# Which work TensorE takes first, where the float limit runs, and which queue loads q and k

## The chip, the cores and the metric

The kernel runs on one core of a Trainium2 chip. TensorE (PE) multiplies matrices into PSUM. VectorE (DVE), ScalarE (ACT) and GpSimd (POOL) do elementwise work, and SyncE (SP) does nothing here but issue DMAs. Each engine has its own stream of instructions and takes them in the order in which the program lists them; an instruction waits on semaphores until its inputs are there. The metric is the device time in microseconds (us) of one execution; the lower the better.

## The reference, cut to what matters

The input is q, k and v of 8 batches, 8 heads, 576 tokens and 64 dimensions, and four weight matrices in float64.

```python
scores = scale * np.matmul(q, k.transpose(0, 1, 3, 2))
thresh = np.max(scores, axis=-1, keepdims=True) - tau
scores = np.where(scores >= thresh, scores, -1000000000.0)
scores = scores - np.max(scores, axis=-1, keepdims=True)
attn = np.exp(scores)
attn = attn / (np.sum(attn, axis=-1, keepdims=True) + 1e-09)
x = (attn @ v), laid out as (8, 576, 512)

xt = x.transpose(0, 2, 1)
h = np.maximum(xt @ w_tok1, 0.0) @ w_tok2
u = x + h.transpose(0, 2, 1)
h2 = np.maximum(u @ w_ch1, 0.0) @ w_ch2
return u + h2
```

## The kernel before

**Attention.** A batch is called a row, and two heads of it are a pair, so there are 8 rows of 4 pairs, numbered 0 to 31. Pair 6 is the third pair of row 1. A unit is 128 queries with both heads of a pair (18 units a row). For two units at a time PE computes scores (`scores_of_two`, L752) into two large PSUM buffers. DVE takes the maxima (`top`, L765), POOL makes the bias (`shift`, L770), ACT applies threshold and scale (`mask`, L780) and the exponential (`exps`, L790), DVE inverts the sums (`inverse`, L276 and L277), and POOL scales the weights (`scale`, L284). The scaled weights must be transposed. In row 0 PE does that through PSUM banks (`turn`, L299, copied out at L304). From row 1 on DVE transposes blocks of 32 x 32 (`turn_blocks`, L314), and four DMAs a unit move the blocks to their place (`move`, L326). Then PE multiplies with v, three units at a time (`values`, L364 for its first matmuls and L369 for the others), and ACT or DVE copies the result out (L373).

**Loads.** A pair's q and k come in eight DMAs of 72 KB (`load_qk`, L106) into two pairs of buffers, so a load must wait until DVE has transposed the pair two before (`prep`, L269). v comes in one DMA in row 0 (`load_v`, L117) and in four later (L120), and its middle part is split off for `values` (`split_middle`, L340). All these DMAs, the moves, the weight loads (L200), the turns of the output (L847), the stores (L895) and the spills (L482) are issued on SP, one after the other.

**Weights.** float64 becomes float32 during row 0, in 31 pieces. ACT prepares two halves (L215, L217), then comes the float limit, a maximum and a multiplication (`on_vector` part 0, L225), then two bit operations on DVE (L227, L231) and an integer addition on POOL (L239). The raw buffer of a piece is loaded anew only when that addition is done.

**MLP.** When a row's attention is done, PE has its token MLP (L398, L410, L423, with adds on DVE at L434) and one or two groups of its channel MLP (L855, its relu at L860 on ACT or L863 on DVE; L871, copied out at L885 or L891). These small products go through two PSUM banks, and fill PE between the scores and the values of the next row. What is put off is done after the attention by hand-written code with fewer products (L1214).

**The planner.** The order of instructions on each engine is found while the program is built, by a greedy planner (`Scheduler`, L518 on). Each operation has an engine, a planned cost, a rank (a lower one goes first), and the operations that it depends on. `start` gives the earliest time at which an operation could begin by the plan. `pick` (L560) takes, for each engine, the operation that can start first; among those that can start now, the one of the lowest rank:

```python
c = (t, rank, x.index) if t > now + 0.02 else (now, rank, x.index)
```

`transfer` plans DMAs: each takes its issue time on the issuing engine, moves at a planned rate, and lands 1.5 us after. At most eight are in flight. An operation may name a second engine (`other`), and then the engine that could start it earlier gets it. What the planner emits is fixed: on the chip an engine that comes to an instruction whose inputs are late waits there, whatever else could run.

Of the kernel before, what the change touches and what calls it, by code (L numbers as in the profile page):

```python
# [14 lines left out]
ALU = mybir.AluOpType  # L15
# [6 lines left out]
def kernel(  # L22
# [25 lines left out]
    nc = tc.nc  # L48
# [10 lines left out]
    NP = H // 2  # L59
# [156 lines left out]
            else:  # L216
                nc.scalar.activation(out=h2, in_=hi.bitcast(F32), func=AF.Abs)  # L217

    def on_vector(i, part, on=nc.vector):
        if wide(i):  # L220
            dst = pieces[i][0]
            lo, hi, h2 = raws[i]
            bits = dst.bitcast(U32)
            if part == 0:
                on.tensor_scalar(out=h2, in0=h2, scalar1=2.0**-15, scalar2=2.0**16, op0=ALU.max, op1=ALU.mult)  # L225
            elif part == 1:
                nc.vector.tensor_scalar(  # L227
                    out=bits, in0=h2.bitcast(U32), scalar1=3, scalar2=0, op0=ALU.logical_shift_left, op1=ALU.bitwise_or
                )
            else:  # L230
                nc.vector.scalar_tensor_tensor(  # L231
                    out=bits, in0=hi, scalar=0x80000000, in1=bits, op0=ALU.bitwise_and, op1=ALU.bitwise_or
                )
# [262 lines left out]
        nc.vector.tensor_scalar(out=ntau, in0=toff, scalar1=SCALE, scalar2=None, op0=ALU.mult)  # L496

    TOKEN_RANK, TOKEN_AFTER_TOKEN = 1.5, 2.5
    FLIGHT, RATE, LANDING = 8, 214.0, 1.5

    class Op:
# [15 lines left out]
    class Scheduler:  # L517
# [22 lines left out]
        def banked(self, cost, work, on, cost_out, leave, deps=(), rank=5, row=None, rank_out=0, other=None):  # L540
# [3 lines left out]
            y.frees = x  # L544
            return x, y

        def start(self, x, eng):
            t = max([d.landed or d.end + (d.lag if d.eng != eng else 0.0) for d in x.deps] + [0.0])
            if x.dmas and len(self.in_flight) == FLIGHT:
                t = max(t, self.in_flight[0])  # L550
            if x.shared and eng == "dve":
                t = max(t, self.clock["pool"])
            if x.bank:
                frees = [b.free for b in self.banks if b.free is not None]
                if not frees:
                    return None
                t = max(t, min(frees))
            return max(t, self.clock[eng])

        def pick(self, eng):  # L560
            best = None
            now = self.clock[eng]
            held = None
            for x in self.ready[eng]:
                t = self.start(x, eng)
                if t is None:
                    continue
                rank = x.rank
                if rank == TOKEN_RANK and self.last_rank == TOKEN_RANK:
                    rank = TOKEN_AFTER_TOKEN  # L570
                c = (t, rank, x.index) if t > now + 0.02 else (now, rank, x.index)
                if x.rank == 1 and eng == "pe" and self.done < x.plan:
                    held = c, t, x
                    continue
                if best is None or c < best[0]:
                    best = c, t, x
            if held and (best is None or best[0][0] > held[0][0] + 0.3):
                best = held
            return best
# [52 lines left out]
    sched = Scheduler()  # L632
# [3 lines left out]
    def key_op(*key):  # L636
        return keyed.get(key)

    def put(key, x):
        keyed[key] = x  # L640
        return x
# [17 lines left out]
    def put_dv(i, part):  # L659
        before = key_op("pool", 26) if part == 1 and i >= CONV - 2 else None  # L660
        put(
            ("dv", i, part),
            sched.op(
                "dve",
                (0.46, 0.47, 0.62)[part],
                lambda: on_vector(i, part),
                (key_op("ac", i, 1), key_op("dv", i, part - 1), before),
                CR[2],
                other=("pool", 0.64, lambda: on_vector(i, 0, nc.gpsimd)) if part == 0 else None,
                shared=part < 2,  # L670
            ),
        )
# [11 lines left out]

    PREP, LOADS = 0.70, 8

    def rank_of_group(b, p0, g):
        return ((b * NP + p0) // 2) * 3 + g  # L690
# [11 lines left out]
    def make_pair(n):  # L702
        b, p = pairs[n]
        if n:
            ahead = (key_op("prep", n - 2, 0), key_op("prep", n - 2, 1))
            for lo in range(0, LOADS, 2):
                put(
                    ("load", n, lo),
                    sched.op(
                        "sp",  # L710
                        0.9,
                        lambda lo=lo: load_qk(n, (nc.sync,) * 2, range(lo, lo + 2)),
                        ahead,
                        0,
                        after=(key_op("load", n - 1, LOADS - 2),),
                        dmas=(2, 107, 0.45),
                    ),
                )
            slot = last_round(n - 2) if n > 1 else -1
            for which in (1, 0):  # L720
                put(
                    ("prep", n, which),
                    sched.op(
                        "dve",
                        PREP,
                        lambda which=which: prep(n, ((which, 0, S // 32),)),
                        [key_op("load", n, lo) for lo in range(0, LOADS, 2)] + [key_op("S", slot)],
                        3,
                        after=(key_op("prep", n - 1, 0),),
                    ),  # L730
                )
        free = key_op("V", last_values(n - 4)) if n >= VL else None
        if n > 1:
            put(("loadv", n), sched.op("sp", 2.0, lambda: load_v(n), (free,), 0, after=(key_op("loadv", n - 1),), dmas=(4, 70, 0.5) if n >= NP else (1, 280, 0.5)))
        put(("split", n), sched.op("dve" if n >= NP else "pool", 0.25 if n >= NP else 0.5, lambda: split_middle(n), (key_op("loadv", n), free), 2))


# [88 lines left out]
    def make_groups(b, halves):  # L826
        uT = xTs[b]
        reads = []
        for i in range(NOW[b]):
            s = {}  # L830
            n, nt = GR, GR // P
# [67 lines left out]
            if b:  # L899
                turn = sched.op("dve", 1.2, turn_u, have + state["stores"] + state["adds"] + (converted if b == 1 else []), 5)  # L900
                reads.append(turn)
                moved = [sched.op("sp", 1.2, lambda k=k, m=move_u: m(k), (turn,), 1, dmas=(nt, 53, 0.6)) for k in range(4)]
            relus = []
            for j in range(NJ):
                x, y = sched.banked(
# [90 lines left out]
    def make_round(it):  # L996
# [25 lines left out]
        for u in us:  # L1022
            b, p0, t = units[u]
            for h in range(2):
                put(("exp", u, h), sched.op("act", 0.77, lambda u=u, h=h: exps(u, h), (key_op("pre", u, h),), 2, lag=0.3))
            n = sched.op("dve", 0.38, lambda u=u: inverse(u), (key_op("exp", u, 0), key_op("exp", u, 1)), 2)
            s = sched.op("pool", 1.46, lambda u=u: scale(u), (n,), 1)
            deps = [s]
            G = rank_of_group(b, p0, t // GU)
            if not b:  # L1030
                deps += [key_op("V", G - 2) if t % GU == 0 else None, key_op("T", u - 1)]
                for third in range(3):
                    x, y = sched.banked(
                        0.33,
                        lambda bank, u=u, third=third: turn(u, third, bank),
                        "act",
                        0.4,
                        lambda bank, u=u, third=third: turned(u, third, bank, nc.scalar.copy),
                        deps,
                        0,  # L1040
                        other=("dve", 0.5, lambda bank, u=u, third=third: turned(u, third, bank, nc.vector.tensor_copy)),
                    )
                    put(("turned", u, third), y)
                    deps = [x]
                put(("T", u), x)
                if t % GU == GU - 1:
                    make_group(b, p0, t // GU)
                    if t // GU == 2 and p0:
                        rows_due.append(b)
                continue  # L1050
            deps += [key_op("T", u - 1), key_op("M", u - 3)]
            put(("T", u), sched.op("dve", 1.31, lambda u=u: turn_blocks(u), deps, 4))
            put(
                ("M", u),
                sched.op(
                    "sp",
                    2.4,
                    lambda u=u: move(u),
                    (key_op("T", u), key_op("V", G - 2) if t % GU == 0 else None),
                    0,  # L1060
                    after=(key_op("M", u - 1),),
                    dmas=(4, 147, 0.6),
                ),
            )
            if t % GU == GU - 1:
                make_group(b, p0, t // GU)
                if p0 == NP - 2 and t // GU == 2:
                    rows_due.append(b)
# [324 lines left out]
```

## Time and profile before

| | |
|---|---|
| Three runs | 1335.69, 1334.21, 1328.55 us; median 1334.21 us |
| Profiled execution | 1338.39 us; span from the first to the last instruction 1336.6 us |
| Granted TensorE clock, mean | 0.978 of full speed |
| Busy share of the span | PE 94%, DVE 58%, ACT 42%, POOL 30% |
| DMA issues of q and k (L106) on SP | 256 |
| DMA issues of moves (L326) on SP | 504 |
| Float limits (L225) | 26 on POOL, mean 1833 ns; 5 on DVE, mean 923 ns |

The busy shares are means over stages that differ: row 0 with the conversion of the weights until about 190 us, the rows 1 to 7 with MLP work between until about 965 us, and the put-off products until the end. A wait of PE in the profile is the idle time just before an instruction, with what ended it. Where several things were waited for, the profile names the one that came last, and with DMAs that can be a neighbour of the transfer that mattered. PEclk is the granted clock of TensorE as a share of full speed. "SPq" marks instructions of SP's queue, where the duration is that of the issue and not of the transfer.

### The profile page before, as it was taken

To read this page: it belongs to the slowest core of one execution; us is meant where nothing else is said; L and a number is where in the kernel's file an instruction comes from. 1 tells how busy PE (TensorE), PEld (TensorE's weight loads), DVE (VectorE), ACT (ScalarE), POOL (GpSimd) and SP (SyncE) were. 2 spreads that over 40 slices of the span, in tenths; PEclk is the share of its full clock that TensorE was granted. 3 is DMA by queue.
4 is the path that set the end of the run, shared out by engine and by line. 5 is a ranking of instruction groups with operands and counts; after the bars stand their busy time and mean duration, and the time that the engine had idled before them with its cause. 6 is when DMAs were issued, how large, how long until landed. Compare 5 with 4: busy or idle time off the path is not lost.

```text
span 1336.6 us, 21896 instructions
## 1 busy us (share of the span) xinstructions
PE 1255.2 (94%) x7982; PEld 995.2 (74%) x7982; DVE 776.8 (58%) x1418; ACT 567.6 (42%) x1233; POOL 401.7 (30%) x692
## 2 busy tenths in 40 slices
PE   6878979999989999989999999999999999999998
PEld 4555668778657776766776676687988888888887
DVE  5887875374756666774666667664154443444342
ACT  5886654454655465553545446452020211112020
POOL 5987863132332333332332333330000000000100
PEclk7989989999999999998999999999999999999999
DMA  9454775364776676685656576452020201021011
GB/s 169 115 138 106 195 168 138 75 133 119 175 166 127 159 148 141 155 172 116 145 133 141 120 175 148 112 137 83 9 71 17 67 28 32 24 62 26 32 32 32
DMA packets 307195, 145.12 MB, mean 109 GB/s; under 512 B 206672, under 2 KB 299856, under 8 KB 307088
## 3 DMA queue, kind: packets, MB, share of 16 engines
q1 hardware_dynamic: 305216, 143.51, 46.4%
q8 instruction: 63, 1.03, 0.3%
q10 hardware_dynamic: 1872, 0.21, 0.1%
q14 instruction: 44, 0.36, 0.1%
HBM read 47.32 MB, written 13.50 MB: 46 GB/s over the span
## 4 chain that ended last, share of the span: by engine, by line
PE 67%; DVE 9%; SPq 9%; POOL 6%; DMA 5%; issue 2%; ACT 2%; DVEq 0%; ACTq 0%; POOLq 0%
PE bank L871 10%; PE o L1214 10%; PE sc L752 7%; PE bank L855 7%; PE bank L369 6%; PE hx L1214 6%; SPq L326 5%; PE hmm L1214 4%; PE oz L1214 4%; PE hz L1214 4%; PE bank L410 4%; DVE mx L765 3%; PE bank L423 3%; POOL e L284 3%; POOL high L225 2%
## 5 line engine op out<-in xcount | busy, mean ns | idle before, releaser
L284 POOL TENSOR_SCALAR e<-e,rr 128x576 f32<-128x576 f32 x288 | 213.1, 755 | 255.2 <-DVE rr L277 192.0
L780 ACT ACTIVATE e<-sc,bias 128x576 f32<-128x576 f32 x288 | 197.9, 742 | 214.7 <-DVE mx L765 144.6
L765 DVE TENSOR_REDUCE mx<-sc 128x1 f32<-128x576 f32 x288 | 198.0, 746 | 56.5 <-PE sc L752 56.0
L790 ACT ACTIVATE e<-e,ntau 128x576 f32<-128x576 f32 x288 | 220.7, 779 | 0.1
L752 PE MATMUL sc<-kT,qT 64*128 64x192 f32 (+1 forms) x1920 | 174.9, 342 | 18.6 <-ACT e L780 16.8
L314 DVE STREAM_TRANSPOSE T<-e 128x1152 f32<-128x1152 f32 x126 | 171.8, 1369 | 30.9 <-DMA eT<-T 19.9
L871 PEld LDWEIGHTS bank<-wc,g 128*128 128x128 f32 x1536 | 179.0, 193 | 12.6 <-issue 3.9
L855 PE MATMUL bank<-xT,wc 128*128 128x256 f32 x768 | 180.6, 385 | 6.2 <-DVE g L863 5.6
L871 PE MATMUL bank<-wc,g 128*128 128x128 f32 x1536 | 182.2, 276 | 0.8 <-DVE us L885 0.8
L752 PEld LDWEIGHTS sc<-kT,qT 64*128 64x128 f32 (+1 forms) x1920 | 143.9, 181 | 51.1 <-ACT e L780 23.4
L855 PEld LDWEIGHTS bank<-xT,wc 128*128 128x128 f32 x768 | 141.3, 190 | 39.1 <-DVE g L863 9.7
L770 POOL TENSOR_SCALAR bias<-mx,toff 128x1 f32<-128x1 f32 x288 | 78.2, 276 | 242.2 <-DVE mx L765 239.1
L369 PE MATMUL bank<-eT,lv 128*64 128x384 f32 (+1 forms) x1024 | 145.8, 427 | 0.1
L1297 POOL TENSOR_TENSOR us<-us,ut 128x256 f32<-128x256 f32 x27 | 22.4, 844 | 392.9 <-DVE us L1135 392.9
L369 PEld LDWEIGHTS bank<-eT,lv 128*64 128x64 f32 x1024 | 80.6, 143 | 54.9 <-issue 42.3
L423 PE MATMUL bank<-w,a 128*128 128x192 f32 (+1 forms) x256 | 72.7, 418 | 6.8 <-DVE xT L434 5.9
L410 PE MATMUL bank<-x_sb,w 128*128 128x512 f32 (+1 forms) x180 | 74.1, 562 | 0.4 <-ACT eT L304 0.2
L364 PE MATMUL bank<-eT,vl 128*64 128x384 f32 (+1 forms) x256 | 46.1, 438 | 25.2 <-DMA eT<-T 9.1
L1262 ACT ACTIVATE ga<-hmm 128x256 f32<-128x256 f32 x30 | 11.5, 384 | 117.1 <-PE hmm L1214 117.1
L423 PEld LDWEIGHTS bank<-w,a 128*128 128x128 f32 x256 | 42.5, 190 | 23.6 <-DVE xT L434 7.3
L790 ACT ACTIVATION_READ_ACCUMULATOR e<-e,ntau 128x1 f32 x288 | 58.7, 204 | 0.0
L1135 DVE TENSOR_TENSOR temps<-hx,temps 128x256 f32<-128x256 f32 x60 | 25.1, 419 | 56.7 <-PE hx L1214 56.6
(130 smaller groups left out, 1551.7 us busy)
## 6 DMA issues: line engine op xcount, KB each, us to landing
eT<-T SPq DMA_DIRECT2D x504, 144.0 KB, 3.0
lk<-in_k_dram SPq DMA_DIRECT2D x126, 72.0 KB, 3.0
lq<-in_q_dram SPq DMA_DIRECT2D x124, 72.0 KB, 3.1
out_dram<-us SPq DMA_DIRECT2D x32, 256.0 KB, 2.1
ut<-us SPq DMA_DIRECT2D x128, 64.0 KB, 2.1
lv<-in_v_dram SPq DMA_DIRECT2D x112, 72.0 KB, 2.6
spare<-in_moe_w_ch_dram SPq DMA_DIRECT2D x8, 512.0 KB, 3.7
extra<-in_moe_w_ch_dram SPq DMA_DIRECT2D x8, 512.0 KB, 3.8
```

Of the source, the lines that this page charges most:

```text
L284: nc.gpsimd.tensor_scalar(out=eh, in0=eh, scalar1=rr[:, h : h + 1], scalar2=1.0, op0=ALU.mult, op1=ALU.mult)
L314: nc.vector.transpose(out=T.rearrange("p a (c x) -> p c a x", c=NK), in_=e.rearrange("p (c a x) -> p c a x", c=NK, a=4))
L369: nc.tensor.matmul(to[r], lhsT=lv[:, j, :], rhs=e[j], start=False, stop=(c == NI - 1), skip_group_check=True)
L410: nc.tensor.matmul(bank[:, 0 : P * L], lhsT=w1[:, t, P * m : P * m + P], rhs=x_sb[:, t, cols], start=(t == 0), stop=(t == NT - 1))
L423: nc.tensor.matmul(bank[:, n * i : n * i + n], lhsT=hidden[b][:, m, P * c : P * c + P], rhs=w2[:, m, lo : lo + n], start=(m == 0), stop=(m ...
L752: nc.tensor.matmul(sc[h][rows, f, HT * k : HT * k + HT], lhsT=qT[r, cols], rhs=kT[r, HT * f : HT * f + HT], start=True, stop=True, skip_gr ...
L765: nc.vector.tensor_reduce(out=mx[:, h : h + 1], in_=part[h], axis=AX.XY, op=ALU.max)
L780: nc.scalar.activation(out=eh, in_=part[h], func=AF.Prelu, bias=bias[:, h : h + 1], scale=SCALE, alpha=STEEP)
L790: nc.scalar.activation(out=eh, in_=eh, func=AF.Exp, bias=ntau, accum_out=rs[:, h, 0:1])
L855: nc.tensor.matmul(bank[:, 0:n], lhsT=wc1[:, j, c, :], rhs=uT[:, c, GR * i : GR * i + n], start=(c == 0), stop=(c == NCC - 1))
L871: nc.tensor.matmul(to, lhsT=s["g"][:, j, P * t : P * t + P], rhs=wc2[:, j, P * c : P * c + P], start=(j == 0 and b > 0), stop=(j == NJ - 1 ...
L1214: nc.tensor.matmul(ps, lhsT=l, rhs=r, start=start and x == 0, stop=x == len(pairs) - 1, skip_group_check=not start)
```

## The change

1. In `pick`, among the operations that could start now on PE, those that are *sure* go before those that aren't, ahead of the rank. An operation is sure when what it needs lies far enough back in the plan: 1 us (`SLACK`) after the planned end of an operation on another engine, 4 us (`SPARE`) after the planned landing of a DMA, 1 us after the planned release of a PSUM bank.
2. Planned issue times per DMA become longer: 0.58 us for q and k (0.45), 0.67 for v from row 1 on (0.50), 0.645 for moves and for the turns of the output (0.60).
3. The float limit no longer has POOL as its second engine: all 31 are on DVE.
4. From pair 6 on, q and k are loaded by DMAs that ACT issues, two to an operation, at rank 2.5. No ACT operation of the attention has a higher number, so these go last among those that could start now. Earlier pairs stay on SP.

```diff
-    def on_vector(i, part, on=nc.vector):
+    def on_vector(i, part):
...
-                on.tensor_scalar(out=h2, in0=h2, scalar1=2.0**-15, scalar2=2.0**16, op0=ALU.max, op1=ALU.mult)
+                nc.vector.tensor_scalar(out=h2, in0=h2, scalar1=2.0**-15, scalar2=2.0**16, op0=ALU.max, op1=ALU.mult)
...
+    SLACK, SPARE = 1.0, 4.0
...
+        def sure(self, x):
+            t = max([d.landed + SPARE if d.landed else d.end + d.lag + SLACK * (d.eng != x.eng) for d in x.deps] + [0.0])
+            if x.bank:
+                t = max(t, min(b.free for b in self.banks if b.free is not None) + SLACK)
+            return t
...
-                c = (t, rank, x.index) if t > now + 0.02 else (now, rank, x.index)
+                c = t if t > now + 0.02 else now, eng == "pe" and self.sure(x) > now + 0.02, rank, x.index
...
-                other=("pool", 0.64, lambda: on_vector(i, 0, nc.gpsimd)) if part == 0 else None,
...
-    PREP, LOADS = 0.70, 8
+    PREP, LOADS, ONACT = 0.70, 8, NP + 2
...
-                        "sp",
+                        "act" if n >= ONACT else "sp",
                         0.9,
-                        lambda lo=lo: load_qk(n, (nc.sync,) * 2, range(lo, lo + 2)),
+                        lambda lo=lo: load_qk(n, (nc.scalar if n >= ONACT else nc.sync,) * 2, range(lo, lo + 2)),
                         ahead,
-                        0,
+                        2.5 if n >= ONACT else 0,
                         after=(key_op("load", n - 1, LOADS - 2),),
-                        dmas=(2, 107, 0.45),
+                        dmas=(2, 107, 0.58),
...
-            put(("loadv", n), sched.op("sp", 2.0, lambda: load_v(n), (free,), 0, after=(key_op("loadv", n - 1),), dmas=(4, 70, 0.5) if n >= NP else (1, 280, 0.5)))
+            put(("loadv", n), sched.op("sp", 2.0, lambda: load_v(n), (free,), 0, after=(key_op("loadv", n - 1),), dmas=(4, 70, 0.67) if n >= NP else (1, 280, 0.5)))
...
-                moved = [sched.op("sp", 1.2, lambda k=k, m=move_u: m(k), (turn,), 1, dmas=(nt, 53, 0.6)) for k in range(4)]
+                moved = [sched.op("sp", 1.2, lambda k=k, m=move_u: m(k), (turn,), 1, dmas=(nt, 53, 0.645)) for k in range(4)]
...
-                    dmas=(4, 147, 0.6),
+                    dmas=(4, 147, 0.645),
```

## The prediction, made before the changed kernel was run

> **What bounds the kernel now.** I read the windows first, in three stages: row 0 with the weight conversion, rows 1 to 7 of the attention with the MLP work between, and the closing product.
>
> ```profile
> core 0: us, PE busy (x) PEld busy (x) DVE busy (x) ACT busy (x) POOL busy (x), PEclk, DMA share, GB/s
> 0.00:200.00 200.00, 158.59 (x1063) 114.18 (x1065) 153.89 (x289) 139.83 (x290) 154.08 (x213) 0.91 0.66 149
> 200.00:960.00 760.00, 725.76 (x5171) 554.12 (x5168) 463.03 (x836) 373.32 (x814) 225.22 (x452) 0.98 0.58 133
> 960.00:1336.00 376.00, 370.85 (x1752) 326.91 (x1750) 159.87 (x295) 54.45 (x130) 22.41 (x27) 1.00 0.14 38
> ```
>
> TensorE is the bound. The change leaves its work alone, so it can win only what PE idles (41 us before 200, 34.2 from 200 to 960) and what the half clock costs. The last stage is code after the planner and nearly full: nothing there. Next, PE's waits from 200 to 960:
>
> ```profile
> PE bank L364 <- DMA eT<-T: 9.1, 4, 4.5
> PE bank L364 <- DMA lq<-in_q_dram: 5.8, 2, 4.2
> PE bank L423 <- DVE xT L434: 5.1, 3, 2.3
> PE bank L364 <- DMA out_dram<-us: 4.0, 2, 2.0
> ```
>
> L364 is the first matmul of `values`. With its smaller rows (2.4, 2.3, 0.7, 0.2) it makes 24.5 of the 34.2 us, in 12 stalls. The releaser named is only the transfer that landed last; the timeline before the longest stall shows what PE waited for:
>
> ```profile
> 594.06 0.50 SPq L106 DMA_DIRECT2D lk<-in_k_dram  x1
> 594.65 3.04 SPq L120 DMA_DIRECT2D lv<-in_v_dram  x4
> 597.80 5.11 SPq L326 DMA_DIRECT2D eT<-T  x8
> 602.96 1.55 PE L364 MATMUL bank<-eT,vl 128*64 128x384 f32 x4 [4.50 <-DMA eT<-T]
> ```
>
> Eight loads of q and k (589.7 to 594.6, L106) and four of v sat on SP ahead of the eight moves that `values` needed. PE had been sent to `values` because the planner thought that data was there. The clock after such stalls, in windows:
>
> ```profile
> 370.00:374.00 4.00, 3.27 (x12) 1.55 (x14) 0.00 (x0) 0.89 (x4) 1.43 (x2) 0.57 0.84 186
> 445.00:449.00 4.00, 4.00 (x17) 1.62 (x13) 0.00 (x0) 3.83 (x10) 0.00 (x0) 0.57 0.88 243
> 602.00:609.00 7.00, 6.04 (x20) 2.43 (x20) 0.00 (x0) 0.81 (x3) 1.35 (x2) 0.51 0.34 87
> ```
>
> Three more such stretches (from 663, 779 and 813, at 0.58 to 0.60) follow L364 stalls of 2.26, 1.99 and 2.43 us. Last, the moved instructions by source line:
>
> ```profile
> L225 POOL TENSOR_SCALAR high<-high x26: 1058/1918/2333, 15.6 to 185.1; 128x512 f32<-128x512 f32 x22, 128x288 f32<-128x288 f32 x3, 64x256 f32<-64x256 f32 x1
> L225 DVE TENSOR_SCALAR high<-high x5: 427/875/1470, 14.4 to 169.8; 128x512 f32<-128x512 f32 x4, 128x288 f32<-128x288 f32 x1
> L106 SPq DMA_DIRECT2D lq<-in_q_dram x130: 312/535/1762, 1.7 to 825.7; - x130
> L106 SPq DMA_DIRECT2D lk<-in_k_dram x126: 312/497/2069, 0.7 to 826.2; - x126
> L106 ACTq DMA_DIRECT2D lk<-in_k_dram x2: 425/502/580, 0.7 to 1.2; - x2
> ```
>
> The float limit takes POOL about 1.9 us where the planner books 0.64, which is why it sent 26 of 31 there. The planner books 0.45 for a q or k issue that takes 0.5 to 0.54, and 0.50 for a v issue that takes 0.62 (median of L120).
>
> **The change part by part.** The sum goes against the profiled execution, 1338.4 us (span 1336.6 and 1.8 around it); it lies 4.2 above the median of the runs, 1334.2.
>
> A, the L364 stalls. From pair 6 on, 26 pairs x 8 = 208 issues leave SP: 208 x 0.52 = 107 us, 4.1 per pair. By medians SP carries per row 72 moves x 0.60 + 32 loads x 0.52 + 16 v x 0.62 + 8 turned outputs x 0.60 = 75 us of the row's 109 (760 / 7); 58 remain, and moves no longer stand behind eight loads. Then the ordering: `values` counts as sure only 4 us after its planned landing, and among ops that could start now a sure one goes first. All 12 stalls are at most 4.5 us, so the margin covers nearly every one, if PE has sure work then. It usually has: 889 to 967 is leftover MLP work, so the supply lasts. The truer issue times also bring plan and chip together (8 x 0.07 + 4 x 0.12 = 1 us per pair). Bounds: 8 us (only what q and k loads blocked directly, the two longest stalls) to 24.5 (all). I take 17: with two banks, not every stall has a sure op beside it.
>
> B, the half clock. The six stretches lose 4 x (0.43 + 0.43 + 0.42 + 0.41 + 0.40) + 7 x 0.49 = 11.8 us, all behind L364 stalls. In proportion to A, 17 / 24.5 x 11.8 = 8; bounds 3 and 11.8. The Trainium skill (TensorE: Matmul & The Clock Gate, Part 1) has the clock fall only after an idle window of about 3.4 us. By that only the stalls of 4.22 and 4.50 would count, B's ceiling would be 1.7 + 3.4 = 5.1, and the sum about 4 us smaller; the trace shows half clock behind stalls of 2.0 us, so the measurement decides.
>
> C, other late waits: 34.2 - 24.5 = 9.7 us, bank copies and adds on DVE (L434, L863, L885). A bank counts as sure 1 us after its planned release, so the shorter waits go: 3, bounds 0 and 7.
>
> D, row 0. POOL gives up 26 x 1.83 = 47.6 us of its 154. DVE takes 26 x 0.92 = 24 (11 to 38 by its shortest and longest). Of the chain of waits before 200, L225 on POOL is 13.8%, 27.6 us, so some 15 of them; on DVE they would be 15 x 0.92 = 14, net 13.6. DVE was busy 154 of 200 and becomes the tighter engine, and PE's idle after the first 13.5 us is 34.2. I take 9; bounds 20 gained (over half of that idle) and 10 lost (38 more on DVE makes 192 of 200, and score maxima queue behind conversions).
>
> E, the cost on ScalarE. 208 issues x 0.50 (its own four rows at the start) = 104 us on an engine that is busy 373 of 760. They have the lowest rank on ACT and go into its idle time. But ACT is in order: each op is two issues, 1.0 us, and a load first waits for VectorE's transposes of the pair two before (L269). Behind it stand masks (L780), on which score banks wait, exps, and the relus and copies (L860, L373, L402) that free the two MLP banks. Half of PE's bank copies can go to VectorE instead, and the planner books the time. I take 6 lost: 104 ops, one in nine costing PE 0.5 us; bounds 0 and 52 (half of the ops a full 1 us). If the cover is gone, all 104 us show.
>
> The issue durations and removed option add no instruction. Sum: -17 - 8 - 3 - 9 + 6 = -31, so 1338.4 - 31 = 1307.4 profiled, and 1303 at the median.
>
> **Rivals.** *ScalarE pays it back (slower).* Loads stop ACT while PE waits for a mask or a bank. It decides when a two-issue op costs PE on average over 37 / 104 = 0.36 us. At E's upper bound, 52: 1338.4 - 37 + 52 - 4.2 = 1349. For: two MLP banks only, and ACT already waits 132.7 us for score maxima, so it has no lead over DVE. Against: ACT idles 387 of 760, and PE's waits from 200 to 960 show no row on ACT at all. 0.13. With row 0 lost to DVE (D at +10, C at 0, A and B at their low bounds, E at 16, one op in three costing 0.5: -11 + 26 = +15, also 1349): 0.06.
>
> *Transfers, not issues, hold the moves (no change).* The DMA engines were 0.73 busy from 592 to 603 and 0.91 from 364 to 371, and a move lands 3.0 us after issue. Then eT lands no sooner from an emptier SP, and sure work only shifts the stall: A 5, B 2, E 6, rest 0: 1333. Against: at 598 the moves were issued late, not slow. 0.09. The Trainium skill (DMA: Bandwidth & Descriptors, Issuing engines are not separate DMA queues) says that a second issuing engine saves only issue time and that this is usually small. Here issue fills two thirds of SP, so I keep A.
>
> *The ordering hardly bites.* If at most stalls no sure op is ready, only SP's relief and the limit count: A 8, B 4, C 0, D 9, E 6: -15, 1319. 0.20.
>
> **Numbers.** Forecast 0.52, small gain 0.20, no change 0.09, slower 0.19. About 0.5% (6.7 us) is what a measurement of this kernel can tell from no change; so faster 0.72, same 0.09, slower 0.19. All gains at their bounds would be 62 us; I end the range at 1282, and at 1344 above, which holds the milder half of the slower cases. The forecast's own range is 1285 to 1317.
>
> **What would show it.** A: from 200 to 960, PE's waits at the first `values` matmul fall from 24.5 to under 10, and SP's timeline has no L106 after pair 5. B: granted clock of that stage 0.99 or more. D: no limit on POOL, POOL under 110 us busy before 200, PE idle there near 30. E: ACT shows about 208 issues of 0.5 us, and PE's waits on ACT stay under 10. I am wrong if these waits pass 40 us, if L364 keeps its stalls though SP is emptier, or if DVE is busy over 185 of the first 200 us.

## The result, and the profile after

The changed kernel takes 1330.1 us in the median of 22 runs (1326.4 to 1335.1), the kernel before 1334.0 on the same chip: a ratio of 0.997, 95% interval 0.9958 to 0.9981. That is 3.9 us, where 31 had been forecast. The profiled execution took 1331.8 us, its span 1330.0.

The same three stages, in the windows of the changed kernel (columns as before):

```profile
core 0: us, PE busy (x) PEld busy (x) DVE busy (x) ACT busy (x) POOL busy (x), PEclk, DMA share, GB/s
0.00:200.00 200.00, 158.34 (x1102) 114.32 (x1104) 162.49 (x332) 146.19 (x307) 112.57 (x197) 0.92 0.71 161
200.00:960.00 760.00, 726.86 (x5185) 557.83 (x5182) 459.88 (x835) 358.82 (x783) 222.38 (x442) 0.98 0.58 130
960.00:1330.00 370.00, 365.12 (x1702) 321.16 (x1700) 159.16 (x293) 54.45 (x130) 22.41 (x27) 1.00 0.14 38
```

PE idles 41.7 us before 200 and 33.1 from 200 to 960, against 41.4 and 34.2 before, at nearly the same clock. POOL has given up 41.5 us before 200 and VectorE has taken 8.6, and PE has nothing of it. From 200 to 960 the idle time has the same size and other causes. These are the longest of PE's waits there:

```profile
PE bank L398 <- ACT x_sb L402: 10.1, 4, 4.3
PE bank L861 <- ACT g L866: 7.3, 3, 5.9
PE bank L861 <- ACT xT L373: 5.1, 1, 5.1
PE sc L758 <- ACT e L786: 4.7, 5, 1.4
PE bank L877 <- DVE x_sb L402: 2.8, 1, 2.8
```

The rows at L364, 24.5 us before, add up to 2.0. In their place PE waits for ScalarE: with the small rows 28.8 us, and not one such row stood in the kernel before. (The new lines moved the old L752, L780, L855, L860 and L871 to L758, L786, L861, L866 and L877.)

The timeline before the longest of these stalls shows what ScalarE did. An issue has the letter q, and the number in brackets is idle time:

```profile
674.41 0.77 ACT L796 ACTIVATE e<-e,ntau 128x576 f32<-128x576 f32 x1
...
675.07 0.37 ACTq L106 DMA_DIRECT2D lk<-in_k_dram  x1
...
676.89 2.92 POOL L284 TENSOR_SCALAR e<-e,rr 128x576 f32<-128x576 f32 x4 [5.74 <-DVE rr L276]
678.40 1.38 DVE L314 STREAM_TRANSPOSE T<-e 128x1152 f32<-128x1152 f32 x1 [1.12 <-POOL e L284]
...
679.80 2.48 SPq L326 DMA_DIRECT2D eT<-T  x4
...
682.54 0.34 ACTq L106 DMA_DIRECT2D lq<-in_q_dram  x1
683.37 0.34 ACTq L106 DMA_DIRECT2D lk<-in_k_dram  x1
686.59 0.32 ACTq L106 DMA_DIRECT2D lq<-in_q_dram  x1
...
687.59 1.37 ACT L786 ACTIVATE e<-sc,bias 128x576 f32<-128x576 f32 x2 [12.31 <-DMA lk<-in_k_dram]
...
690.04 1.22 PE L861 MATMUL bank<-xT,wc 128*128 128x256 f32 x2 [5.86 <-ACT g L866]
```

The last issue of the first group ends at 675.4, and the next begins at 682.54, 7.1 us later. In the trace it waits for semaphore 105, which it will raise itself. The DMA that used 105 before it is the first move of the four that SP issues at 679.80; it lands at 682.51. The load at 683.37 waits the same way for the second move (landed 683.35), and the one at 686.59 for the fourth (686.57). SP could not issue these moves sooner: POOL scales the weights from 676.89 and VectorE transposes them from 678.40, and both come after exponentials of ScalarE. So ScalarE stands still for transfers that follow from its own work. All that time the masks and the relu for which PE waits stand behind the loads.

Over the whole trace, 207 of ACT's 212 loads wait before they issue for a semaphore of the eight, 100 to 107, by which DMAs of both queues report their landing in turn. ACT stands still before 64 of them, 123 us in all, summed as the idle time on ACT over 0.15 us in front of such an issue. Every one of the 64 stops ends within 0.03 us after the landing of the DMA that used the same semaphore before. For 45 of them that is a move of SP (82 us), for 8 a load of v (19 us), and for only 4 a load of ACT's own; the other 7 (18 us) are weight loads, turns of the output and stores. The Trainium skill (DMA: Bandwidth & Descriptors, Why a DMA increments its semaphore by 16 and not by 1) says why nobody may share one freely: with two DMAs in flight on a semaphore, a wait on its count can pass before the first has fully landed. The trace agrees in that no load issues before the predecessor on its semaphore has landed.

The half clock came along, now behind stops of ScalarE:

```profile
380.00:387.00 7.00, 4.86 (x23) 4.86 (x24) 0.31 (x2) 5.50 (x11) 0.00 (x0) 0.51 0.59 89
687.00:694.00 7.00, 3.96 (x10) 2.77 (x12) 0.46 (x3) 5.92 (x13) 1.42 (x2) 0.52 0.58 134
796.00:803.00 7.00, 3.52 (x8) 2.52 (x8) 0.32 (x2) 6.01 (x14) 0.84 (x2) 0.53 0.89 163
```

The moved instructions by source line, limit and loads:

```profile
L225 DVE TENSOR_SCALAR high<-high x31: 278/419/760, 14.4 to 188.4; 128x512 f32<-128x512 f32 x26, 128x288 f32<-128x288 f32 x4, 64x256 f32<-64x256 f32 x1
L106 ACTq DMA_DIRECT2D lk<-in_k_dram x106: 317/508/1548, 0.7 to 827.0; - x106
L106 ACTq DMA_DIRECT2D lq<-in_q_dram x106: 317/318/1851, 1.8 to 826.6; - x106
```

The limit costs VectorE 0.42 us, not 0.92. The issues cost ACT what was booked or less. Neither is the trouble.

### The profile page after: what moved, and what is told of

It reads as the page before. It is cut to its first block, busy times and chain, and to the rows that moved or that the text cites. A ratio compares the mean times of both kernels' runs of the same rounds, so it can differ in the third digit from the quotient of the medians.

```text
span 1330.0 us, 21951 instructions
## 1 busy us (share of the span) xinstructions
PE 1250.3 (94%) x7982; PEld 993.3 (75%) x7982; DVE 781.5 (59%) x1458; ACT 559.5 (42%) x1219; POOL 357.4 (27%) x666
## 4 chain that ended last, share of the span: by engine, by line
PE 75%; DMA 8%; DVE 7%; ACT 5%; SPq 2%; issue 2%; POOL 1%; ACTq 1%; DVEq 0%; POOLq 0%
PE bank L877 12%; PE o L1220 10%; PE sc L758 9%; PE bank L861 7%; PE bank L369 7%; PE hx L1220 6%; PE bank L410 5%; PE bank L423 4%; PE hz L1220 4%; PE oz L1220 4%; PE hmm L1220 4%; DVE mx L771 3%; DMA eT<-T 3%; ACT e L786 2%; PE bank L364 2%
## 5 line engine op out<-in xcount | busy, mean ns | idle before, releaser
L284 POOL TENSOR_SCALAR e<-e,rr 128x576 f32<-128x576 f32 x288 | 215.2, 763 | 271.4 <-DVE rr L277 239.8
L786 ACT ACTIVATE e<-sc,bias 128x576 f32<-128x576 f32 x288 | 197.2, 744 | 211.2 <-DVE mx L771 79.3
L861 PE MATMUL bank<-xT,wc 128*128 128x256 f32 x768 | 185.3, 393 | 15.0 <-ACT g L866 9.5
L758 PE MATMUL sc<-kT,qT 64*128 64x192 f32 (+1 forms) x1920 | 176.3, 343 | 22.3 <-ACT e L786 20.9
L877 PEld LDWEIGHTS bank<-wc,g 128*128 128x128 f32 x1536 | 182.2, 195 | 12.9 <-DVE x_sb L402 3.0
L877 PE MATMUL bank<-wc,g 128*128 128x128 f32 x1536 | 185.0, 278 | 3.0 <-DVE x_sb L402 2.8
L758 PEld LDWEIGHTS sc<-kT,qT 64*128 64x128 f32 (+1 forms) x1920 | 145.2, 182 | 55.2 <-ACT e L786 27.0
L861 PEld LDWEIGHTS bank<-xT,wc 128*128 128x128 f32 x768 | 145.5, 195 | 46.3 <-ACT g L866 12.1
L369 PE MATMUL bank<-eT,lv 128*64 128x384 f32 (+1 forms) x1024 | 135.8, 408 | 0.0
L369 PEld LDWEIGHTS bank<-eT,lv 128*64 128x64 f32 x1024 | 74.3, 138 | 51.2 <-issue 45.8
L276 DVE TENSOR_REDUCE rr<-rs 128x2 f32<-128x4 f32 x144 | 21.7, 151 | 110.3 <-ACT e L796 109.7
```

The source lines that it names most:

```text
L284: nc.gpsimd.tensor_scalar(out=eh, in0=eh, scalar1=rr[:, h : h + 1], scalar2=1.0, op0=ALU.mult, op1=ALU.mult)
L369: nc.tensor.matmul(to[r], lhsT=lv[:, j, :], rhs=e[j], start=False, stop=(c == NI - 1), skip_group_check=True)
L758: nc.tensor.matmul(sc[h][rows, f, HT * k : HT * k + HT], lhsT=qT[r, cols], rhs=kT[r, HT * f : HT * f + HT], start=True, stop=True, skip_gr ...
L786: nc.scalar.activation(out=eh, in_=part[h], func=AF.Prelu, bias=bias[:, h : h + 1], scale=SCALE, alpha=STEEP)
L861: nc.tensor.matmul(bank[:, 0:n], lhsT=wc1[:, j, c, :], rhs=uT[:, c, GR * i : GR * i + n], start=(c == 0), stop=(c == NCC - 1))
L877: nc.tensor.matmul(to, lhsT=s["g"][:, j, P * t : P * t + P], rhs=wc2[:, j, P * c : P * c + P], start=(j == 0 and b > 0), stop=(j == NJ - 1 ...
```

## The experiments

Times are medians; a ratio is to runs of the kernel before on the same chip (1330.7 to 1333.5 us), with its 95% interval.

**One part undone: loads back on SP.** Everything else of the change stays.

```diff
-    PREP, LOADS, ONACT = 0.70, 8, NP + 2
+    PREP, LOADS, ONACT = 0.70, 8, 10**9
```

> The changed kernel with one part undone: all loads of q and k are issued on SP again (rank 0), and everything else stays (sure work first, new issue durations, limit on VectorE). Theory 1 (stalled ScalarE): in the changed kernel ACT stands still for 123 us before its load issues, each of which waits for a semaphore that an earlier DMA, mostly of SP, must raise; that is where PE's new waits on ACT from 200 to 960 come from (about 29 of 33 us) and the 8.6 us stop at 185. Then without loads on ACT those waits are under 8 us, some 3 to 10 us of waits at the first values matmul come back because SP is full again, and the time is 1295 to 1315. Theory 2 (the order moved the stalls): sure work first itself made PE run into late PSUM banks. Then PE's idle from 200 to 960 stays near 33 us, on banks, and the time is 1325 to 1335.

1280.9 us, ratio 0.9613 (0.9591 to 0.9634): 50 us faster than before, and faster than both theories said. In its windows and in its waits from 200 to 960:

```profile
0.00:200.00 200.00, 172.59 (x1266) 129.63 (x1268) 165.05 (x336) 150.60 (x320) 114.92 (x203) 0.97 0.74 169
200.00:960.00 760.00, 748.43 (x5258) 578.38 (x5259) 478.43 (x866) 368.21 (x802) 219.05 (x437) 1.00 0.58 131
```

```profile
PE bank L364 <- DMA eT<-T: 2.7, 2, 2.1
PE bank L364 <- DVE g L869: 2.0, 1, 2.0
...
PE bank L861 <- ACT xT L373: 0.6, 1, 0.6
```

PE idles 27 us before 200 and 12 after, at a clock of 0.97 and 1.00. Waits for ScalarE are under 2 us. The loads on ScalarE alone cost 0.997 - 0.961 of 1332 us, about 48 us, and that is where the forecast gain went. So it is not true that the ordering as such moved the stalls (theory 2).

**One part alone: loads on ScalarE** (the fourth part of the change, added to the kernel before).

> The kernel before with one part of the change alone: loads of q and k from pair 6 on are issued on ACT, with the old planned durations. Theory 1: ACT stands still for 100 us or more before its load issues; PE waits on ACT for 20 to 40 us more from 200 to 960, while its waits at the first values matmul fall from 24.5 to 10 to 20 us because SP has fewer issues; time 1335 to 1360, slower than before. Theory 2: ACT is not at fault, so the emptier SP shows: 1315 to 1328.

1337.6 us, ratio 1.0038 (1.002 to 1.0057): slightly slower. ACT stops for 122 us before 83 of its loads. The waits at `values` do fall, from 24.5 to under 7 us, but PE waits 26 us for ACT:

```profile
PE sc L752 <- ACT e L780: 7.7, 7, 2.4
PE bank L364 <- ACT g L860: 5.6, 2, 3.5
PE bank L398 <- ACT x_sb L402: 4.0, 4, 1.3
PE bank L871 <- ACT xT L373: 3.7, 1, 3.7
```

So the waits that an emptier SP was to remove fall by some 17 us, and ScalarE takes back more. Whether the emptier SP alone did that isn't shown, for while ScalarE stands still the moves have more time as well. With sure work first and truer durations, waits at `values` fall just as far with the loads on SP (24.5 to 6.9), and the whole cost of the stops is left. That would be why this part costs 5 to 7 us here and 48 there.

**One part alone: the limit on VectorE.**

```diff
-                other=("pool", 0.64, lambda: on_vector(i, 0, nc.gpsimd)) if part == 0 else None,
```

> The kernel before with one part of the change alone: the float limit always on VectorE. POOL's busy time before 200 falls from 154 to about 112 and VectorE's rises from 154 to about 162. Theory 1 (row 0 gains, and the stop at 185 in the changed kernel hid it): PE's idle before 200 falls from 41 to 28 to 36 us, time 1322 to 1330. Theory 2 (row 0 is not bound by POOL): idle before 200 stays at 39 to 44, time 1330 to 1338.

1313.7 us, ratio 0.9859 (0.9837 to 0.9881).

```profile
0.00:200.00 200.00, 172.20 (x1234) 127.18 (x1234) 167.63 (x344) 155.25 (x328) 117.84 (x207) 0.94 0.73 167
```

PE idles 28 us before 200 in place of 41, at 0.94 in place of 0.91: theory 1, and more than it said. In the changed kernel ACT's stops take it back in the same stretch (PE idles 41.7 us there, and 27 with the loads back on SP): PE waits 8.6 us at 184.7 for a mask while ACT stands before three loads (3.0, 2.2 and 3.2 us).

**One part alone: sure work first** (`SLACK`, `SPARE`, `sure` and the new line of `pick`, added to the kernel before).

> The kernel before with one part of the change alone: sure work first on TensorE, with the old issue durations and loads on SP. Theory 1: the ordering alone removes most waits at the first values matmul (24.5 to under 8 us), and with them most of the half clock; time 1305 to 1320. Theory 2 (the order moved the stalls): the same us come back as waits on PSUM banks copied out by ACT or VectorE; time 1328 to 1338.

1315.1 us, ratio 0.987 (0.9848 to 0.9892). The time is in theory 1's range, but the step is not: 18 us of waits at `values` remain, most of them in three stalls:

```profile
PE bank L364 <- DMA eT<-T: 13.5, 3, 5.4
```

A margin of 4 us did not keep PE from stalls of up to 5.4 us. Whether the plan was off by more than the margin there, or no sure work was left, this run alone does not tell.

**One part alone: the new issue durations** (0.58, 0.67 and 0.645 for 0.45, 0.50 and 0.60).

> The kernel before with one part of the change alone: the new planned issue durations. With sure work first and the limit they were worth 28 us (1309.0 to 1280.9). If truer durations help on their own, waits at the first values matmul fall from 24.5 to under 16 and the time is 1312 to 1325. If they only help together with the margins of the sure rule (what is left of the error must be smaller than the margin), the time is 1326 to 1338.

1298.7 us, ratio 0.9744 (0.9721 to 0.9766), faster than either guess: four numbers of the planner that add no instruction are the largest single part.

```profile
200.00:960.00 760.00, 745.45 (x5327) 580.27 (x5326) 472.71 (x853) 375.96 (x824) 221.41 (x444) 1.00 0.58 134
```

PE idles 14.6 us from 200 to 960 in place of 34.2, the clock is full, and waits at `values` are 8 us. TensorE's work is the same in both kernels, so this is all idle time and half clock. The order that the planner finds is one of many, and how far these 35 us hang on it was not tried; but the six kernels here that have sure work first, the limit and the new numbers, with loads on SP and no stops of ScalarE, have orders of their own and lie within 1275 to 1282 us.

**Sure work and limit, old durations** (the kernel with loads on SP, with the four old numbers).

> The kernel before with sure work first and the limit on VectorE, but with the old planned issue durations and all loads on SP. Alone the two parts gave -16 and -17 us, and all three without ACT loads -50. Theory A (truer issue durations bring the missing 17): 1294 to 1304, with 12 us or more of waits at the first values matmul from 200 to 960. Theory B (durations hardly matter, the two parts help each other): 1277 to 1287, these waits under 9 us.

1309.0 us, ratio 0.9824 (0.9796 to 0.9852), 28 us above the kernel with the new numbers, with 16.5 us of waits at `values`: theory A in the mechanism, though the cost was larger than it said. With the old durations the margin alone doesn't cover the plan's error.

**Occupied time without waits.** To the kernel with loads on SP (1280.9 us), four copies for each of the 104 load operations (the buffer that they copy is left out here):

```diff
+                if n >= NP + 2:
+                    sched.op("act", 1.16, lambda: [nc.scalar.copy(out=idle_work, in_=idle_work) for _ in range(4)], ahead, 2.5)
```

> The kernel with all loads on SP at rank 0 (1280.9 us), and in addition, for each of the 104 load operations of the changed kernel, four small copies on ACT at the same rank 2.5 and with the same dependences (about 1 us of ACT each, planned at 1.16 like the two issues). ACT gets the occupied time of the issues without their waits. Theory 1 (standing still for semaphores costs the time, occupation does not): PE's waits on ACT from 200 to 960 stay under 8 us, time 1279 to 1292. Theory 2 (the occupied time delays masks and bank copies): these waits reach 18 us or more, time 1312 to 1332.

1281.8 us, ratio 0.9616 (0.9597 to 0.9635), not to be told from 1280.9, though ACT is 84 us busier from 200 to 960:

```profile
L716 ACT COPY idle_work<-idle_work x416: 227/244/323, 106.2 to 771.8; 128x64 f32<-128x64 f32 x139
```

416 copies of 0.244 us are 101 us of ACT, as much as the loads' issues in the changed kernel (98 us). PE waits for ACT 1.4 us. Planned work of lowest rank is hidden; theory 2 falls.

**Waits without issues, first try.** To the kernel with loads on SP, for each of the 104 load operations, one copy of two columns on ACT that reads what the moves of two units before brought (`moves_made[0]`; the planner doesn't know that).

```diff
...
+            tile_, place = moves_made[0]
+            nc.scalar.copy(out=idle_work, in_=tile_[:, place, k, 0:2])
...
```

> The kernel with all loads on SP at rank 0 (1280.9 us), and in addition, for each of the 104 load operations of the changed kernel, one tiny copy on ACT (2 columns, about 0.2 us, rank 2.5) that reads what the moves of two units before have brought, so that ACT waits until that move, eight to eleven DMAs back in the order of the moves, has landed. The planner does not know of that wait. ACT gets the waits of the loads without their issues. Theory 1 (waiting for other DMAs' landing is enough to cost the time): ACT stops for 40 us or more at these copies, PE's waits on ACT from 200 to 960 reach 10 us or more, time 1292 to 1330. Theory 2 (the waits alone are harmless; it takes a load issue): PE's waits on ACT stay under 6 us, time 1278 to 1288.

1280.5 us, ratio 0.9615 (0.9594 to 0.9636). This tells nothing on the question: ACT never stopped, since those moves had always landed.

**Waits without issues, second try.** The copies read the move issued last (`moves_made[-1]`).

> As the run before (tiny copies on ACT that read what a move has brought, loads on SP), but each copy now reads the move issued last, not the one of two units before. With that one ACT never stopped: all those moves had landed. Theory 1: ACT now stops for 60 us or more at the 104 copies, PE's waits on ACT from 200 to 960 reach 10 us or more, time 1292 to 1330. Theory 2 (these waits are harmless even when they happen): ACT stops as long, PE's waits on ACT stay under 6 us, time 1278 to 1288.

1327.2 us, ratio 0.9953 (0.9937 to 0.9969). By the copies' tile, what ACT waited for before them (us, times); then PE's waits from 200 to 960:

```profile
L339 ACT COPY idle_work<-eT x96: 183/192/210, 146.1 to 817.8; 128x2 f32<-128x2 f32 x96
its engine sat idle before it (us, times) until:
  DMA eT<-T: 129.0, 43
```

```profile
PE bank L407 <- ACT x_sb L411: 9.0, 4, 4.0
PE sc L769 <- ACT e L797: 5.8, 4, 3.7
PE bank L872 <- ACT g L877: 5.1, 2, 4.7
PE bank L872 <- ACT xT L382: 3.5, 1, 3.5
```

Without one load on ACT from pair 6 on, 129 us of waits for moves to land bring back the same picture as in the changed kernel, with the same four rows at the top (all rows on ACT make 28.6 us, 28.8 there), and cost some 45 us. The waits alone are enough: theory 1.

**Loads on ACT, later in the plan.** A load is placed only 4 us after the planned landing of the second of the eight DMAs before it.

```diff
+                if eng == "act":
+                    t = max(t, self.in_flight[1] + 4.0)
```

> The changed kernel, all its loads still on ACT, but the planner places one only 4 us after the planned landing of the DMA that used its second completion semaphore before. Same issues on the same engine, only the waiting in front of them goes. Theory 1 (ACT loses the time by standing still for semaphores that other DMAs raise): ACT's stops before load issues fall from 123 us to under 40, PE's waits on ACT from 200 to 960 from 29 to under 10, time 1283 to 1300. Theory 2 (the 98 us of issuing on ACT are what delays masks and bank copies): PE's waits on ACT stay at 18 us or more, time 1312 to 1332.

1333.1 us, ratio 1.0009 (0.999 to 1.0027). Inconclusive: the stops fell from 123 to 90 us only, in 34 places, and PE still waits 24 us for ACT. 24 of these stops, 74 us, end with a move of SP, so on the chip those moves land later than the plan and the margin allow for. Waits at `values` are back too, 17 us with one of 11.3, so the remedy has a price of its own.

**Loads issued by POOL**, from pair 6 on.

> The changed kernel with the loads from pair 6 on issued on POOL, which is busy 222 of the 760 us from 200 to 960 and frees no PSUM bank. Theory 1 (any in-order engine that issues these loads stands still; it matters by who waits for it): ACT has no stops, but POOL delays biases and scalings; PE has spare work, so less reaches it: 1285 to 1315. Rival: these DMAs hold POOL for far longer than the 0.5 us that they hold ACT, biases come late, ACT waits for POOL by 80 us or more, time above 1330.

1294.9 us, ratio 0.9718 (0.9683 to 0.9754).

```profile
L106 POOL DMA_DIRECT2D lq<-in_q_dram x104: 665/674/864, 90.1 to 775.3; - x104
```

An issue takes POOL 0.67 us, but POOL stands idle before only one of them, for 0.4 us: its loads report on eight other semaphores (111 to 118), which no move uses. PE waits for ACT 0.4 us from 200 to 960. So loads on POOL's queue, which don't share the eight semaphores, bring no stops. By the medians POOL costs some 14 us over SP. The profiled execution was the fastest of the five (1287.9 us) and shows 6 of them, before 200: there PE idles 32 us in place of 27, at a clock of 0.92 in place of 0.97.

**Toward a faster version: loads on SP at rank 2.5,** so that moves and v go first.

> The changed kernel with the loads of q and k on SP, but still at the low rank 2.5, so that moves, v and stores that could be issued at the same time go first. With the loads on SP at rank 0 the time was 1280.9 us. If what is left at the first values matmul there (6.9 us) comes from loads ahead of moves, it falls under 4 and the time is 1272 to 1279. If the loads now come so late that scores wait for them, VectorE waits for q and k by 15 us or more and the time is 1285 to 1300.

1276.3 us, ratio 0.9578 (0.9548 to 0.9608), as expected if loads stood ahead of moves: PE idles 7.8 us from 200 to 960, and 3.5 are left at `values`. The gain over 1280.9 is small, and the two ratios' intervals overlap. With wider margins (`SLACK, SPARE = 1.5, 6.0`) on top:

> The kernel with loads on SP at rank 2.5 (1276.3 us) with wider margins: 1.5 us for engines and banks, 6 us for transfers. From 200 to 960 PE idles 7.5 us there, so at most that is to be had: 1270 to 1276. If the wider margin makes too much work unsure, so that the rule no longer tells apart, waits at the first values matmul come back: 1279 to 1290.

1280.1 us, ratio 0.9601 (0.9581 to 0.9622): no gain; 5.6 us of waits at `values` came back. With v also behind the moves (rank 0.5 in place of 0), and the margins as they were:

> The kernel with loads on SP at rank 2.5 (1276.3 us), with the loads of v also behind the moves (rank 0.5 in place of 0). If the last waits at the first values matmul (3.5 us) come from v loads ahead of moves: 1271 to 1275. If v then comes late, VectorE waits longer for it before the split and PE for values: 1278 to 1290.

1275.3 us, ratio 0.9563 (0.9547 to 0.9579), not to be told from 1276.3, with 3.5 us at `values` again. It has the lowest median of all, 58 us under the kernel before.

## Why the prediction was wrong, step by step

**The step that failed is E,** the cost on ScalarE: 6 us by the sum, with a bound of 52; the runs show about 48. The prediction named the right place: ACT in order, and behind the loads the masks, relus and copies for which PE waits. It named the wrong wait. That "a load first waits for VectorE's transposes of the pair two before" is known to the planner, and none of the 64 stops ended with it. What stopped ACT was the semaphore of an earlier DMA, mostly a move of SP, that had not landed. The planner does count at most eight DMAs in flight, but by its own landing times; on the chip ACT came to 64 of its loads before the landing. The trace of before has such waits on most of SP's issues, but there they stand in one queue behind the very DMAs that they wait for, and from 100 to 900 us no stop of SP ends with one. I took the price of an issue from four unhindered ones at the start of the kernel, and asked what the occupied time costs; the dummy copies show that this costs nothing. The price of a wait was never worked out.

Between the profiled executions of the changed kernel (span 1330.0 us) and of the one with loads on SP (1280.4), TensorE's work is the same. They differ by 36 us in which PE idles, 14 of them before 200 us, and by 14 us that PE is busy longer, at the half clock. E had neither the stops in row 0 nor the half clock behind stops. As for the signs, PE's waits on ACT from 200 to 960 passed the 10 us that were named, at 28.8, but not the 40.

**The rival was the right one, with too low a chance.** "ScalarE pays it back" had 0.13, and its turning point was 0.36 us of PE per two-issue operation. Measured: 48 / 104 = 0.46. It came out at 1330 and not at 1349, because the gains were some 50 us and not 37, and E 48 and not 52. That the two nearly cancel is chance.

**A: the size was right, the means were not.** Waits at `values` fell from 24.5 to 2.0 us in the changed kernel, under the 10 that was asked for, and no load of q or k is issued by SP after 63.5 us. But with the loads left on SP they fell as well, to 6.9: 17.6 us, where I took 17, though SP keeps all its loads. Nor did the margin cover "nearly every one" of the stalls: sure work first alone left 18 us. What I had put in one sentence, that truer issue times "bring plan and chip together", is the largest part: alone it leaves 8 us of these waits, and the kernel takes 35 us less.

**B: right, and hidden.** One minus the granted clock, summed over the time from 200 us to the closing product, is 11.9 us before and 3.4 with loads on SP: 8.5, where I took 8. In the changed kernel it is 13.7, behind the new stops, and the clock of that stage stayed at 0.98, so B didn't show.

**D: right on its own, 17 us where I took 9.** PE idles 13.6 us less before 200, and the half clock costs 11.9 us there in place of 17.1, which the prediction had not counted in row 0. The price of the limit on VectorE was 0.42 us, less than half of the 0.92 that I took from five rows. The slow rows had company on POOL: of the four with 512 columns, the one with nothing beside it took 0.43 us, one beside a scaling (L284) 0.88, and two beside the integer addition (L239) 1.27 and 1.47. POOL's 112.6 us before 200 came near the 110 forecast; PE's idle there, forecast near 30, is 28 alone and 41.7 in the changed kernel.

**C was not told apart** by any run: PE's other idle time from 200 to 960, 9.7 us before, is 4.7 with loads on SP, 5 less where I took 3, but which part did it is open.

**Transfers, not issues, hold the moves** was a wrong rival: with loads on SP and truer numbers, a move lands 3.0 us after its issue, as in the kernel before (the engines' share is 0.58 in both), and most of the stalls are gone (24.5 to 6.9 us).

Together A to D were forecast at 37 us and are worth some 50 (1280.9). The surplus lies before 200 us: with loads on SP, PE idles 14 us less there and loses 10 us less to the half clock (17.1 to 6.8), where the prediction had 9 in all. E takes 48 of them. One sum was off: the gains at their bounds make 63 us and not 62, on which nothing hangs.

## What to carry to other kernels

Before a DMA is moved to a compute engine's queue, look at what each issue waits for, not only at what it takes: a wait that costs nothing on an engine that only issues stops everything behind it on one that computes. If two queues share a few completion semaphores in turn, each waits for the other's DMAs, late ones included. And where a program plans its own order, compare the planned durations with the trace first: here four numbers were worth more than the rule built to guard against their error.

## What was not expected of the hardware

A maximum and a multiplication over 512 columns take GpSimd 1.96 us (mean of 22 in the kernel before), while two multiplications over 576 take it 0.76; VectorE does the first in 0.42 (median in the changed kernel). Beside an integer addition on GpSimd the same instruction took VectorE up to 1.47 us, and a bit operation of 0.42 us (L227) took 1.51 four times. TensorE fell to half clock behind stops of about 2 us (0.57 to 0.60 granted behind stalls of 1.99 to 2.43 us in the kernel before).
